# A Fourier mixing layer with a capped mixture of experts: when the first stage of two sequences runs, which engine copies it, and when its tables are asked for

## The chip, the core and the metric

The kernel runs on one core of a Trainium2 chip. The core has a matrix engine (TensorE, PE in the profile), VectorE (DVE), ScalarE (ACT), GpSimd (POOL), a queue engine (SyncE, SP) and 16 DMA engines that all transfers share. Each engine works through its own list of instructions in order, and waits for the others by semaphores. The metric is the time of one execution on the device, in microseconds (us); the figure for a kernel is the median of several executions. Before the change it is 474.11 us (three runs, 473.17 to 475.94).

## What is computed

Eight sequences of 2496 positions with 256 channels are filtered in the frequency domain, and the result goes through eight experts, each of which keeps at most 80 tokens:

```python
X = np.fft.rfft(x, axis=1)                       # x: (8, 2496, 256)
y = np.fft.irfft(X * (filt_r + 1j * filt_i)[None], n=2496, axis=1)
x = y.reshape(8 * 2496, 256)
logits = x @ w_gate                              # 8 experts
expert_idx = np.argmax(logits, axis=1)
# softmax probability of the chosen expert is the gate;
# of each expert's tokens the 80 with the largest gate are kept
out[tok_idx] = gate_w[tok_idx, None] * (np.maximum(x[tok_idx] @ w1[e], 0) @ w2[e])
```

All other rows of the output are zero.

## The kernel before

The Fourier transform is done by matrix products: 2496 is 39 times 64. The work of a sequence b runs in four stages.

- `stage1(b, k)`, k = 0 to 10 (L299 to L312), transforms over the 39. It reads one half of an x chunk (four row groups, 468 KB, `load_x`), makes eight PE instructions into one PSUM tile `pa` (pool `fps`, three buffers, shared with the next two stages), and copies 480 elements per partition into the tile `t1`, with a stride (L312). Eleven such units make a sequence. `t1` has two buffers, one for a sequence.
- `transpose1(b, u)`, u = 0 to 9 (L314), turns two slices of `t1` on PE and copies them with ScalarE into `t2` (L322).
- `stage2(b, u)` (L326) multiplies by the table `d_t` on PE (L331), by the filter on VectorE (two products, L339), and combines on GpSimd (two instructions, L345). It needs the piece `d(u // 2)` of the table and the filter row pair u in `ft`.
- `turn(b, u)` (L349) transforms over the 64 on PE, adds columns for the expert logits, copies the result with ScalarE (L369) and stores it.

The filter has to be brought into shape once: `load_filter(v, half)` (L265) issues two gathers of 128 KB from the GpSimd queue (half 0 the real part, half 1 the imaginary), `sign_filter(v)` (L273) flips signs in the imaginary part on ScalarE, and `turn_filter(v, k)` (L279) transposes on PE and copies with VectorE. There are five v of them, each for two values of u.

The order of all instructions is written out by hand. At the beginning seven x chunks are asked for on the SP queue (NX0 = 7 buffers; a sequence has NCH = 6 chunks), with the first table piece `load_d(0)` between the sixth and the seventh. GpSimd asks for the filter pieces (0, 0) and (0, 1), clears several tiles, copies two identities, and then executes a one-element copy `mark` that reads the last chunk of sequence 0 (L816); what stands behind it on GpSimd waits until that chunk is there. Behind it are four more filter pieces, (1, 0) to (2, 1), and two small pieces of the gate weights. On PE, `put_s1()` takes the next unit of stage 1 from a list over all sequences, and after every second one asks for one more x chunk (`put_x`), which waits for the buffer of the chunk just used. Eleven units are put first, then filter piece 0 is turned, then two transposes with a unit behind each. Then the loop at L853 runs over v = 10 b + u: stage2 of v, a piece of the filter (in the first eight steps), for v below 4 another `load_filter`, the transpose of v + 2, one unit of stage 1 (two at u = 3), and the turn of v - 2.

Of the kernel before, what the change touches and what calls it, by code (L numbers as in the profile page):

```python
# [27 lines left out]
NU = NS // 2  # L28

NJ, NG = 3, 22  # L30
NB = NG // 2
# [50 lines left out]
def kernel(  # L82
# [11 lines left out]
    nc = tc.nc  # L94
# [94 lines left out]
    def put_zeros(n):  # L189
        for i in zeros[:n]:  # L190
            nc.sync.dma_start(
                out=out[i * ZR:i * ZR + ZR, :].rearrange("r d -> (r d)").rearrange(
                    "(p m) -> p m", p=128),
                in_=zero_t[:])
        del zeros[:n]
# [36 lines left out]
    with ExitStack() as actx:  # L232
# [32 lines left out]
        def load_filter(v, half):  # L265
            k, filt = half, (filt_r, filt_i)[half]
            for i in range(2):
                nc.gpsimd.indirect_dma_start(
                    out=fst[:, v, 2 * k + i, :], out_offset=None, in_=filt[:, :],
                    in_offset=bass.IndirectOffsetOnAxis(  # L270
                        ap=frow[:, 2 * v + i:2 * v + i + 1], axis=0))

        def sign_filter(v):  # L273
            f = fst[:, v]
            for i in range(2):
                nc.scalar.activation(out=f[:, 2 + i, :], in_=f[:, 2 + i, :], func=AF.Copy,
                                     scale=fsig[:, 2 * v + i:2 * v + i + 1])
# [21 lines left out]
        def stage1(b, k):  # L299
            if k == 0:  # L300
                st["t1", b] = t1pool.tile([128, 4 * NS, N2], F32, name=f"t1_{b}", tag="t1")
            xt = st["x", b, 2 * k // JC]
            ps = fps.tile([128, 2, NJ, 4 * NS], F32, name=f"pa_{b}_{k}", tag="f")
            for i in range(2):
                for cb in range(NDB):
                    nc.tensor.matmul(  # L306
                        out=ps[:, i, :, 2 * NS * cb:2 * NS * cb + 2 * NS],
                        lhsT=xt[0:NJ * N1, (2 * k + i) % JC, 128 * cb:128 * cb + 128],
                        rhs=wf_t[:], start=True, stop=True)
            h = k // (NB - 1)  # L310
            t1 = st["t1", b][:, :, h:h + N2 - 1].rearrange("p a (j g) -> p g j a", j=NJ)
            nc.scalar.copy(out=t1[:, 2 * k - h:2 * k - h + 2], in_=ps[:])  # L312

        def transpose1(b, u):  # L314
            t1 = st["t1", b]
            ps = fps.tile([128, 2, NDB, 128], F32, name=f"pt_{b}_{u}", tag="f")
            for i in range(2):
                for cb in range(NDB):
                    a = 2 * NS * cb + 2 * (2 * u + i)
                    nc.tensor.transpose(ps[:, i, cb, :], t1[:, a:a + 2, :].rearrange("p r n -> p (r n)"), ident[:])  # L320
            t2 = t2pool.tile([128, 2, C], F32, name=f"t2_{b}_{u}", tag="t2")
            nc.scalar.copy(out=t2[:].rearrange("p i c -> p (i c)"),  # L322
                           in_=ps[:].rearrange("p i c q -> p (i c q)"))
            st["t2", b, u] = t2
# [456 lines left out]
        LATE, LEAD = 2, 2  # L781
        with tc.manual_schedule():
# [6 lines left out]
            def put_x():  # L789
                if xs:  # L790
                    load_x(*xs.pop(0))

            def put_s1():
                if s1:
                    b, k = s1.pop(0)
                    stage1(b, k)
                    if (2 * k + 2) % JC == 0 or k == NB - 1:
                        put_x()

            def load_d(g):  # L800
                nc.sync.dma_start(out=d_t[:, SG * g:SG * g + SG, :],
                                  in_=d_dram.ap()[:, SG * g:SG * g + SG, :])

            for _ in range(NCH):
                put_x()
            load_d(0)
            for _ in range(NX0 - NCH):
                put_x()
            load_filter(0, 0)
            load_filter(0, 1)  # L810
            for t in (lg, zero_t, *zs, key, kt):
                nc.gpsimd.memset(t[:], 0.0)
            nc.gpsimd.tensor_copy(out=gi[:, 0, E:E + 128], in_=ident[:])
            nc.gpsimd.tensor_copy(out=gi[:, 1, 0:128], in_=ident[:])
            mark = tpool.tile([1, 1], F32, name="mark")
            nc.gpsimd.tensor_copy(out=mark[:], in_=st["x", 0, NCH - 1][0:1, 0, 0:1])  # L816
            load_filter(1, 0)
            nc.gpsimd.dma_start(out=gi[:, 0, 0:E], in_=moe_w_gate[0:128, :])
            nc.gpsimd.dma_start(out=gi[:, 1, 128:128 + E], in_=moe_w_gate[128:256, :])
            load_filter(1, 1)  # L820
            load_filter(2, 0)
            load_filter(2, 1)
            for k in range(NB):
                put_s1()
                if k in (2, 5, 8):
                    load_d(k // 3 + 1)
            sign_filter(0)
            turn_filter(0, 0)
            turn_filter(0, 1)
            for v in range(LEAD):  # L830
                transpose1(0, v)
                put_s1()
            load_d(4)
            nlow = max(128 - cap, 8) // 8
            n0 = max(128 - cap, 8) // 8
            early = {67: [lambda: pick_edge(0, 6, 8, -1.0)],
# [16 lines left out]
            for v in range(B * NU + LATE):  # L853
                b, u = divmod(v, NU)
                if b < B:
                    stage2(b, u)
                    if v + 2 < NU:
                        if v % 2 == 1:
                            sign_filter(v // 2 + 1)
                        turn_filter(v // 2 + 1, v % 2)  # L860
                    if v < 4:
                        load_filter(3 + v // 2, v % 2)
                    elif v == 4:
                        nc.gpsimd.dma_start(out=e_t, in_=e_dram.ap())
                        nc.gpsimd.dma_start(out=wi_t, in_=wi_dram.ap())
                    w = v + LEAD
                    if w < B * NU:
                        transpose1(*divmod(w, NU))
                    put_s1()
                    if u == 3:  # L870
                        put_s1()
                    if b > 0:
                        put_zeros(1)
                if v >= LATE:
                    turn(*divmod(v - LATE, NU))
                if b > 0 and u == LATE:
                    logits(b - 1, 0)
                if b > 0 and b % 2 == 0:
                    if u == LATE + 1:
                        logits(b - 1, 1)  # L880
                    if b < 6 and u in (4, 5, 6, 7, 8, 9):
                        gating(b // 2 - 1, u - 4)
                        if u == 9:
                            gating(b // 2 - 1, 6)
                    elif b == 6 and u in (4, 5):
                        gating(2, 2 * u - 8)
                        gating(2, 2 * u - 7)
                    elif b == 6 and u in (6, 7):
                        gating(2, u - 2)
                        if u == 7:  # L890
                            gating(2, 6)
                for act in early.pop(v, []):
                    act()
                if v == B * NU:
                    turn_rows(0, 0)
                    turn_rows(0, 1)
# [656 lines left out]
```

## Time and profile before

The profile is of one execution.

| what | value |
|---|---|
| median of the runs | 474.11 us |
| the profiled execution | 481.94 us |
| its span, first to last instruction | 480.1 us |
| mean granted TensorE clock | 0.962 |
| PE busy | 442.1 us (92%) |
| weight loads of PE busy | 416.0 us (87%) |
| ACT busy | 222.4 us (46%) |
| DVE busy | 187.9 us (39%) |
| POOL busy | 176.6 us (37%) |
| copy of stage 1 (ACT, 88 of them) | 1000 ns each |
| copy after the transposes (ACT, 80) | 586 ns each |
| product with the filter (DVE, 160) | 681 ns each |
| combination (POOL, 160) | 735 ns each |
| gathers of the filter (POOL issues, 20) | about 950 ns each |

Busy time of an engine is time in which at least one of its instructions runs. Matrix instructions overlap, so PE's mean of one (about 275 ns) is more than the time by which each advances the engine. An entry such as "4.59 <-remote" behind an instruction says how long its engine stood idle before it, and what released it. The page cuts the span into 40 slices of 12 us; the opening that the change touches is the first five of them.

### The profile page before, as it was taken

The page shows a single profiled execution, that of the slowest core. Times are in us where ns is not written, and L with a number is a line of the kernel's source. Part 1 is how long each engine was busy: PE and PEld are TensorE (multiplying, and loading weights), DVE is VectorE, ACT ScalarE, POOL GpSimd, SP SyncE. Part 2 cuts the span into 40 slices and gives each one's busy share as a digit, 9 for nine tenths or more (in the row PEclk, how much of TensorE's full clock was granted, in tenths as well). Part 3 has the DMA queues.
Part 4 walks back from the last instruction along what each step waited for, and adds up shares of the span by engine and source line. Part 5 has one row for each costly group of instructions (what it writes and reads, how often), then busy time and mean ns, then how long its engine had stood idle before and what let it go on. Part 6 is the DMA issues. An engine that isn't in the chain of part 4 may idle for free. (4 is left out here: it accounts for less than half of the span.)

```text
span 480.1 us, 8658 instructions
## 1 busy us (share of the span) xinstructions
PE 442.1 (92%) x3372; PEld 416.0 (87%) x3372; DVE 187.9 (39%) x562; ACT 222.4 (46%) x364; POOL 176.6 (37%) x244
## 2 busy tenths in 40 slices
PE   5869999999999999999999987999889996999990
PEld 5769999999999999999999887888778886888870
DVE  2135553554664455655546995484110000011100
ACT  3835667666766666676667443322123220011110
POOL 7486434443543443444435446103620010211210
PEclk9979999999999999999999999999899996699996
DMA  7995467888778878788961326888779999155000
GB/s 215 279 293 167 151 192 218 246 262 251 250 247 254 268 271 248 203 265 280 401 238 47 132 89 213 311 338 324 283 268 383 379 389 349 53 181 173 20 18 11
DMA packets 38324, 109.95 MB, mean 229 GB/s; under 512 B 4667, under 2 KB 14202, under 8 KB 36760
## 3 DMA queue, kind: packets, MB, share of 16 engines
q1 hardware_dynamic: 26224, 73.26, 46.5%
q10 hardware_dynamic: 8642, 24.19, 13.1%
q0 software_dynamic: 3408, 11.86, 7.4%
q8 instruction: 29, 0.48, 0.4%
q14 instruction: 21, 0.17, 0.1%
HBM read 68.97 MB, written 43.20 MB: 234 GB/s over the span
## 5 line engine op out<-in xcount | busy, mean ns | idle before, releaser
L345 POOL TENSOR_TENSOR p<-p,p 128x256 f32<-128x256 f32 x160 | 114.0, 735 | 139.0 <-DVE p L339 97.2
L339 DVE TENSOR_TENSOR p<-pb,ft 128x512 f32<-128x512 f32 x160 | 102.3, 681 | 13.1 <-PE pb L331 10.7
L306 PE MATMUL pa<-wf_t,x 117*128 117x120 f32 x704 | 93.3, 280 | 6.6 <-DMA x<-in_x_dram 6.6
L312 ACT COPY t<-pa 128x480 f32<-128x480 f32 x88 | 87.0, 1000 | 26.4 <-PE pa L306 26.0
L306 PEld LDWEIGHTS pa<-wf_t,x 117*128 117x128 f32 x704 | 87.4, 197 | 6.9 <-DMA x<-in_x_dram 5.8
L354 PE MATMUL py<-gi,p 128*128 128x136 f32 x640 | 88.1, 280 | 1.3 <-POOL p L345 1.3
L331 PE MATMUL pb<-d_t,t 128*128 128x128 f32 x640 | 86.1, 278 | 0.9 <-DVE p L339 0.8
L354 PEld LDWEIGHTS py<-gi,p 128*128 128x128 f32 x640 | 79.8, 190 | 1.9 <-POOL p L345 1.9
L331 PEld LDWEIGHTS pb<-d_t,t 128*128 128x128 f32 x640 | 78.9, 193 | 1.7 <-DVE p L339 1.0
L322 ACT COPY t<-pt 128x512 f32<-128x512 f32 x80 | 46.9, 586 | 69.4 <-PE pt L320 64.8
L496 PE MATMUL po<-yb,wt 128*128 128x256 f32 x240 | 57.3, 383 | 2.0 <-ACT wt L489 2.0
L496 PEld LDWEIGHTS po<-yb,wt 128*128 128x128 f32 x240 | 43.8, 192 | 7.4 <-ACT wt L489 2.5
L320 PE MATMUL pt<-ident,t 128*128 128x128 f32 x320 | 48.5, 274 | 0.0
L489 ACT COPY wt<-pw 128x512 f32<-128x512 f32 x40 | 23.3, 586 | 54.1 <-PE pw L485 52.4
L374 DVE COPY z<-py 128x16 f32<-128x16 f32 x60 | 11.2, 186 | 91.9 <-ACT ysp L369 57.9
L320 PEld LDWEIGHTS pt<-ident,t 128*128 128x128 f32 x320 | 38.1, 143 | 0.0
L369 ACT COPY ysp<-py 128x512 f32<-128x512 f32 x60 | 35.4, 590 | 0.0
L1129 PEld LDWEIGHTS ph<-xs,w 128*128 128x128 f32 x256 | 32.9, 209 | 1.7 <-DVE xs L1120 1.2
L1129 PE MATMUL ph<-xs,w 128*128 128x80 f32 x256 | 33.1, 293 | 0.8 <-DVE xs L1120 0.8
L1144 PE MATMUL po<-w,hT 128*80 128x256 f32 x128 | 31.2, 402 | 0.0
L485 PE MATMUL pw<-ident,gts 128*128 128x128 f32 x160 | 24.7, 281 | 4.6 <-DMA gts<-rows_tbl,idxb 4.6
L1099 POOL DMA_INDIRECT xg<-y_sel,idxg x8 | 7.7, 962 | 55.9 <-ACT wt L489 40.3
(195 smaller groups left out, 315.7 us busy)
## 6 DMA issues: line engine op xcount, KB each, us to landing
out_dram<-zero_t SPq DMA_DIRECT2D x64, 312.0 KB
x<-in_x_dram SPq DMA_DIRECT2D x40, 468.0 KB
yf<-ysp ACTq DMA_DIRECT2D x30, 512.0 KB
yb<-yf SPq DMA_DIRECT2D x6, 2560.0 KB
w<-in_moe_w_dram SPq DMA_DIRECT2D x14, 1024.0 KB
yf<-ys ACTq DMA_DIRECT2D x10, 512.0 KB
w<-in_moe_w_dram ACTq DMA_DIRECT2D x2, 1024.0 KB
x<-in_x_dram SPq DMA_DIRECT2D x8, 234.0 KB
```

What stands on the lines that cost most here:

```text
L306: nc.tensor.matmul(out=ps[:, i, :, 2 * NS * cb:2 * NS * cb + 2 * NS], lhsT=xt[0:NJ * N1, (2 * k + i) % JC, 128 * cb:128 * cb + 128], rhs=w ...
L312: nc.scalar.copy(out=t1[:, 2 * k - h:2 * k - h + 2], in_=ps[:])
L320: nc.tensor.transpose(ps[:, i, cb, :], t1[:, a:a + 2, :].rearrange("p r n -> p (r n)"), ident[:])
L322: nc.scalar.copy(out=t2[:].rearrange("p i c -> p (i c)"), in_=ps[:].rearrange("p i c q -> p (i c q)"))
L331: nc.tensor.matmul(out=ps[:, cb, i], rhs=d_t[:, 2 * u + i, :], start=True, stop=True, lhsT=t2[:, i, 128 * cb:128 * cb + 128])
L339: nc.vector.tensor_tensor(out=pt, in0=ps[:].rearrange("p c s r q -> p (c s) r q"), in1=f.unsqueeze(2).to_broadcast([128, 2 * NDB, 2, NQ]), ...
L345: nc.gpsimd.tensor_tensor(out=yt[:, :, r, :], in0=yt[:, :, r, :], in1=pr[1][:, :, 1 - r, :], op=op)
L354: nc.tensor.matmul(out=ps[:, i, ZW * cb:ZW * cb + ZW], rhs=gi[:, cb, :], lhsT=yt[:, 2 * cb + i].rearrange("p r q -> p (r q)"), start=True, ...
L369: nc.scalar.copy(out=dst, in_=ps[:, :, E:E + C])
L496: nc.tensor.matmul(pos[t][:, 0, 0:C], lhsT=wts[t, g // 2][:, g % 2, i, :], rhs=ybs[t][:, s, :], start=(s == 0), stop=(s == NS - 1))
L1129: nc.tensor.matmul(ph[:, fc // 4, fc % 4, 0:cap], lhsT=self.w1s[e][:, k, 128 * fc:128 * fc + 128], rhs=xs[:, k, :], start=(k == 0), stop=( ...
L1144: nc.tensor.matmul(po[0:cap, :], lhsT=hT[:, fc, :], rhs=self.w2s[e][:, fc, :], start=(fc == 0), stop=(fc == NFC - 1))
```

## The change

Three things are moved in the opening. All 22 units of sequences 0 and 1 are put as one block before the filter is turned; the loop then puts no units for v = 0 to 7 and goes on as before from v = 8. For these two sequences the copy of a unit goes to VectorE where k is odd. The two filter pieces that GpSimd asked for first stand behind `mark` now, and the five table pieces are asked for during the second half of the block.

```diff
             h = k // (NB - 1)
             t1 = st["t1", b][:, :, h:h + N2 - 1].rearrange("p a (j g) -> p g j a", j=NJ)
-            nc.scalar.copy(out=t1[:, 2 * k - h:2 * k - h + 2], in_=ps[:])
+            copy = nc.vector.tensor_copy if b < 2 and k % 2 else nc.scalar.copy
+            copy(out=t1[:, 2 * k - h:2 * k - h + 2], in_=ps[:])
...
             for _ in range(NCH):
                 put_x()
-            load_d(0)
             for _ in range(NX0 - NCH):
                 put_x()
-            load_filter(0, 0)
-            load_filter(0, 1)
...
             nc.gpsimd.tensor_copy(out=mark[:], in_=st["x", 0, NCH - 1][0:1, 0, 0:1])
+            load_filter(0, 0)
+            load_filter(0, 1)
             load_filter(1, 0)
...
-            for k in range(NB):
+            for k in range(2 * NB):
                 put_s1()
-                if k in (2, 5, 8):
-                    load_d(k // 3 + 1)
+                if NB <= k < 2 * NB - 1 and k % 2:
+                    load_d(k // 2 - NB // 2)
             sign_filter(0)
             turn_filter(0, 0)
             turn_filter(0, 1)
             for v in range(LEAD):
                 transpose1(0, v)
-                put_s1()
-            load_d(4)
...
                     w = v + LEAD
                     if w < B * NU:
                         transpose1(*divmod(w, NU))
-                    put_s1()
-                    if u == 3:
+                    if v >= NU - LEAD:
                         put_s1()
+                        if u == 3:
+                            put_s1()
```

## The prediction, made before the changed kernel was run

> **What bounds the kernel now.** I read the page's slices first, then the stretches of the opening microseconds, then its timeline. Steps are called by their loop index v (one row pair of one sequence); "a unit" is one stage1 (two row groups). The page, one digit per 12 us:
>
> ```profile
> PE   5869999999999999999999987999889996999990
> ...
> PEclk9979999999999999999999999999899996699996
> DMA  7995467888778878788961326888779999155000
> ```
>
> TensorE is full from the fourth slice on. The change lies in the first five slices, where PE has holes, the clock falls once, and the DMA engines are near full for three slices. The answer by stretches (length, busy time of each engine with its instructions, granted clock, DMA share, GB/s):
>
> ```profile
> 13.30:18.80 5.50, 4.70 (x41) 4.55 (x41) 0.00 (x0) 4.41 (x6) 1.43 (x3) 1.00 0.88 264
> ...
> 27.90:31.40 3.50, 0.04 (x2) 0.02 (x1) 1.29 (x2) 1.83 (x4) 3.02 (x5) 0.85 0.93 297
> 31.40:37.20 5.80, 5.80 (x28) 5.70 (x29) 1.08 (x2) 1.90 (x3) 4.00 (x5) 0.50 0.86 261
> 37.20:61.00 23.80, 23.23 (x198) 22.07 (x198) 12.32 (x29) 15.96 (x25) 13.42 (x18) 1.00 0.48 152
> 60.00:260.00 200.00, 199.94 (x1767) 199.48 (x1766) 105.62 (x274) 135.25 (x205) 84.07 (x120) 1.00 0.77 249
> ```
>
> From 60 us on PE is busy 199.94 of 200 us: time won or lost before then reaches the end undiminished. The hole is one stall of 3.5 us and then 5.8 us at half clock. The timeline there, and around the first block:
>
> ```profile
> 5.78 7.54 PE L306 MATMUL pa<-wf_t,x 117*128 117x120 f32 x48 [5.78 <-DMA x<-in_x_dram]
> ...
> 13.78 2.02 PE L306 MATMUL pa<-wf_t,x 117*128 117x120 f32 x16 [0.46 <-DMA x<-in_x_dram]
> ...
> 16.14 2.91 PE L306 MATMUL pa<-wf_t,x 117*128 117x120 f32 x24 [0.34 <-DMA x<-in_x_dram]
> 16.91 0.18 POOL L816 COPY mark<-x 1x1 f32<-1x1 f32 x1 [5.77 <-DMA x<-in_x_dram]
> ...
> 26.86 1.06 PE L331 MATMUL pb<-d_t,t 128*128 128x128 f32 x8
> ...
> 28.28 1.41 POOL L345 TENSOR_TENSOR p<-p,p 128x256 f32<-128x256 f32 x2
> 29.57 0.59 ACT L322 COPY t<-pt 128x512 f32<-128x512 f32 x1 [4.59 <-remote]
> 29.76 1.29 DVE L339 TENSOR_TENSOR p<-pb,ft 128x512 f32<-128x512 f32 x2 [2.31 <-remote]
> ...
> 31.39 1.12 PE L284 MATMUL pf<-ident,fst 128*128 128x128 f32 x4 [3.46 <-ACT fst L276]
> ```
>
> PE waits for sign_filter on ScalarE, and ScalarE stood 4.6 us before a copy whose PE input, by PE's records, was finished at 26.14; VectorE stood too, though its input was finished at 27.92. "Remote" means no instruction of the trace explains the release. No other wait of the trace bears that name. So this stall isn't a dependency of the program.
>
> **What the Trainium skill says.** "TensorE: Matmul & The Clock Gate", What's actually happening: after an idle window of about 3.4 us the clock goes to half. The trace agrees: clock 0.50 right after 3.46 us of idleness, matmul groups 1.90 instead of 1.05 us. "DMA: Bandwidth & Descriptors", Issuing engines are not separate DMA queues: SP's and POOL's transfers share the same 16 engines and interleave. The trace agrees: 250 to 300 GB/s in total whether POOL's gathers run or not. "VectorE: DVE Perf Modes", the errata section's table: a PSUM copy costs 120 + elements cycles at 0.96 GHz, for 480 elements 0.63 us, an estimate; the nearest row here, VectorE's 128x512 PSUM copy, takes 0.69 us.
>
> **The change part by part.** Prices. The iterations at v = 8, 9 start their stage2 at 60.14 and 63.29: 3.15 us for 28 PE operations (stage2 8, transposes 4, stage1 8, turn 8), so 0.90 us for a unit, a stage2 or a turn, 0.45 for a transpose group or a filter turn. PE's work up to stage2 of v = 8 is the same before and after (22 units; thereafter the order is the same instruction for instruction). So I compare one moment: the start of stage2 at v = 8, 60.1 us in the profile.
>
> (1) Block of 22 units. The first six take until 13.3 as now (first x at 5.78, slow until the clock rises). Copies: ScalarE needs 1.00 us a unit, so alone it would hold PE (0.90) back; in turn with VectorE a pair needs 1.0 us against 1.8 of PE. VectorE's strided copy isn't in the trace: from 0.63 to about 1.2 us (ScalarE's strided 480 elements take 1.00, its 512 plain ones 0.59); either end is hidden, so 0. Sixteen units then give 13.3 + 14.4 = 27.7 at best.
>
> (2) Does x come in time? A chunk is 117 x 4 KB = 0.48 MB. Without gathers the x queue moves about 0.28 MB/us (279 and 295 GB/s at 15 to 21). Chunk 4 of sequence 0 landed at 16.14, when some 3.06 MB of that queue had moved (3.65 MB in all less 0.52 gathers and 0.07 small tables) though 2.40 were needed: later transfers interleave, so a chunk lands 0.6 MB late. Moving d(0) and the first four gathers away, chunks 3 and 4 land at about 11.9 and 13.6 (needed 13.3, 15.1) and chunk 5 at 14.5 (16.9 now). From there POOL gathers 128 KB each 1.25 us; their traffic begins about 2.5 us after issue, at 17, and leaves x 0.19 to 0.20 MB/us (total 0.29). At 17, 3.95 MB of 5.87 have moved (5.27 for two sequences, 0.6 late); the rest takes 9.6 us: last chunk at 26.6, just before its use at 26.8, with some 0.4 us lost on the chunk before. I take the block's end E at 28.1; bounds 27.7 and, at 0.17 MB/us, 29.2. SP's later entries x(2,0) and d(0) stand behind; d(0) lands near 30.3, needed at E + 3.4 = 31.5; d(1) needed 4 us later; 0.
>
> (3) POOL. The mark copy at 14.5 instead of 16.9, then 12 gathers x 1.25 + 1.2 for two small DMAs + 0.2: free at 30.9 (28.28 now). Its memsets move ahead from 7.6 to 2.7 us and wait for nothing. Behind the mark's wait for x stand all gathers and the two gate pieces; the filter turns wait for them, first at E, and sequence 0's first product at E + 5.8 = 33.9 finds POOL free: 0.
>
> (4) From E to stage2 of v = 0: turn_filter 0.45; sign_filter waits for ScalarE's last unit copy (1.0) and takes 0.9, so filter turns end at E + 2.2 (the same 2.2 as now between 18.8 and 21.03); two transposes 0.9; without the two units that now lie between, stage2 waits 0.3 for the ScalarE copy of 0.59. Start E + 3.4.
>
> (5) v = 0 to 7 without units. PE's own work: 1.8 each for v = 0 and 1, 2.7 each for six more; odd v lose 0.6 each to sign_filter, as now (the stage2 starts of v = 4 to 8 lie 3.58, 4.18, 3.59 and 4.17 apart). That gives v = 8 at E + 3.4 + 19.8 + 2.4 = E + 25.6. But POOL has 1.41 of products and two gathers (2.23, with gaps 2.44) for each of v = 0 to 3: 3.85 us a step. Its first product ends at E + 7.2 (stage2 0.9, VectorE 1.3, POOL 1.4, latencies), the fifth at E + 7.2 + 4 x 3.85 = E + 22.6, while PE would want it at E + 21.5. The units covered this until now. PE waits about 1.1, shared by v = 5 and v = 6: v = 8 at E + 26.7 = 54.8 us.
>
> Sum: 54.8 against 60.1 in the profile is -5.3 us. But the profiled execution took 481.9 us (span 480.1), 7.8 above the median 474.1, and the stall is worth 3.0 (31.4 instead of 28.4, when the gather for sign_filter would be there, an estimate from its neighbours' landings) and 2.9 (half of 5.8): 5.9. Without it v = 8 stands at 54.2, and the change costs 54.8 - 54.2 = +0.6. I hold the stall for something of the profiled execution: it has no releaser in the program, and it fills most of the 7.8. The cost that replaces the gains: the gain in the block (1.25 us of x waits and copies at 13.3 to 19.05) goes to POOL's 1.1 and the uncovered 0.3 + 0.4.
>
> **Rivals.**
> A. No measurable change, as summed: 474.7; own range 472.8 to 476.8. For it: the "remote" rows and the gap to the median. Chance 0.50.
> B. The stall belongs to the kernel, and the timed runs have it too; units in a block remove it (PE then waits for nothing that is 3.4 us long). -4 to -5.3: about 469.3. For it: DMA share 0.93 to 0.96 through all of 18 to 31, which the change relieves nowhere but reorders. Against: the median. Chance 0.28.
> C. Slower, one mechanism: the filter gathers, now started together beside the second half of the block, starve x(1, 3..5). If x gets 0.15 instead of 0.20 MB/us from 17 us on, the last chunk lands at 29.8, PE idles some 2.6 us in the block, and with sign_filter's 1 us behind it a clock window falls empty: 6.8 us at half clock, 3.4 more. It decides from about 2 us of lateness; 477 without the clock, 480 with it. Against: the x queue kept 0.19 beside gathers between 27 and 36 us. Chance 0.22.
> VectorE as the bound is excluded: 2.34 us an iteration against 2.7.
>
> **How the numbers follow.** A measurement tells about 0.5%, 2.4 us, from no change. Faster: 0.85 of B and a little of A, 0.28. Slower: nine tenths of C and a tenth of A, 0.26. The rest, 0.46, the same. The range 469 to 477.5 leaves out the strongest part of B and the clock case of C.
>
> **What would show it.** In the changed profile: mark at 14 to 15 us; x waits under 1 us in units 12 to 22; block end 27.7 to 29; turn's matmuls waiting for POOL's products at v = 5 and 6; stage2 of v = 8 near 55; no 0.5 clock before 300 us. An end of the block after 30, or half clock before 60, is C; a timed gain over 3 us is B. If products don't hold PE, step 5 was too dear by 1.1.

## The result, and the profile after

The changed kernel takes 475.49 us (median of 20 runs, 471.3 to 481.29); the kernel before, run beside it, 474.50 us (20 runs, 470.89 to 477.71). The recorded ratio is 1.0106, with an interval from 1.0061 to 1.0151: slower, where no measurable change was forecast. A recorded ratio leaves out executions that are over 1.5% above the fastest of their kernel, which are many where times scatter (18 of the 22 of e17, 8 of the 11 of the kernel before beside e9 to e12), so the medians over all executions stand beside it and say more there. Here the medians are only 0.2% apart, and the times on record don't show how a ratio of 1.0106 comes of them, so the size of the loss in this comparison is uncertain. The changed kernel run again on chip 15 (e2, e14) is slower by 1.1 to 1.6% by either measure. The profiled execution took 476.66 us, its span is 474.9 us, its mean granted clock 0.975. Three rows of the changed kernel's page, by slices of 12 us:

```profile
PE   5988899999999999999999997999899997999990
...
PEclk9999999999999999999999999899899998799997
DMA  6899547887778887788962224697959999654000
```

The deep hole of the third slice is gone, and the clock doesn't fall in the opening. (The clock has no record before its first change, at 14.08 us here, and the views show it as full there; a unit's 1.71 us until then, against 0.90 after, shows that PE ran at half.) The stretches of the same profile (length, busy time of PE, weight loads, DVE, ACT and POOL with the instructions of each, granted clock, DMA share, GB/s):

```profile
5.30:14.10 8.80, 8.50 (x38) 8.21 (x39) 1.89 (x4) 1.95 (x2) 0.11 (x1) 1.00 0.83 278
14.10:31.00 16.90, 16.17 (x141) 15.78 (x141) 10.06 (x32) 8.82 (x9) 11.85 (x14) 1.00 0.93 252
31.00:34.40 3.40, 2.22 (x17) 1.55 (x15) 1.46 (x3) 2.27 (x5) 1.19 (x2) 1.00 0.97 263
34.40:59.40 25.00, 21.95 (x177) 19.93 (x178) 16.46 (x34) 11.31 (x22) 18.98 (x25) 1.00 0.73 216
59.40:260.00 200.60, 200.52 (x1773) 200.05 (x1772) 106.20 (x275) 135.44 (x204) 85.12 (x122) 1.00 0.75 245
```

The block is no longer stopped, yet it isn't short either: in its first 8.8 us PE does 38 instructions, fewer than five units, and the loop's 25 us hold 3 us of idle PE. The timeline of the same profile at the places that the prediction named:

```profile
5.30 3.77 PE L306 MATMUL pa<-wf_t,x 117*128 117x120 f32 x16 [5.30 <-DMA x<-in_x_dram]
...
9.10 0.97 DVE L313 COPY t<-pa 128x480 f32<-128x480 f32 x1 [9.10 <-PE pa L306]
9.37 7.85 PE L306 MATMUL pa<-wf_t,x 117*128 117x120 f32 x48 [0.30 <-DMA x<-in_x_dram]
...
15.91 0.18 POOL L814 COPY mark<-x 1x1 f32<-1x1 f32 x1 [10.50 <-DMA x<-in_x_dram]
...
28.03 3.04 PE L306 MATMUL pa<-wf_t,x 117*128 117x120 f32 x24 [0.49 <-DMA x<-in_x_dram]
...
34.44 1.16 PE L332 MATMUL pb<-d_t,t 128*128 128x128 f32 x8 [0.24 <-ACT t L323]
...
48.46 0.44 PE L284 MATMUL pf<-ident,fst 128*128 128x128 f32 x2 [1.70 <-DMA fst<-in_filt_r_dram,frow]
...
59.36 1.05 PE L332 MATMUL pb<-d_t,t 128*128 128x128 f32 x8
```

Stage2 of v = 8 starts at 59.36, where the sum had 54.8. Three terms make the 4.6 us. The clock rose at 14.08 us (9.84 before), so six units ended near 15.4 (the first eight, 64 instructions, end at 17.22, and two take 1.8), not at 13.3: 2.1. The other sixteen took 15.7 to the block's end at 31.07 instead of 14.8: 0.9, of which 0.49 is the wait for x. And the loop took 28.3 from there instead of 26.7, because a filter piece came 1.70 us late at v = 4: 1.6.

### The profile page after: what moved, and what is told of

Same layout as the page of the kernel before. It is cut to its first block, busy times and chain, and to the rows that moved or that the text cites. A ratio compares the mean times of both kernels' runs of the same rounds, so it can differ in the third digit from the quotient of the medians.

```text
span 474.9 us, 8658 instructions
## 1 busy us (share of the span) xinstructions
PE 441.2 (93%) x3372; PEld 414.9 (87%) x3372; DVE 196.9 (41%) x572; ACT 213.9 (45%) x354; POOL 176.1 (37%) x244
## 3 DMA queue, kind: packets, MB, share of 16 engines
q10 hardware_dynamic: 8642, 24.19, 13.2%
## 5 line engine op out<-in xcount | busy, mean ns | idle before, releaser
L313 ACT COPY t<-pa 128x480 f32<-128x480 f32 x78 | 77.6, 1001 | 33.9 <-PE pa L306 33.3
L1128 PE MATMUL ph<-xs,w 128*128 128x80 f32 x256 | 32.3, 289 | 0.8 <-DVE xs L1119 0.8
```

Source lines behind the costliest of these rows:

```text
L1128: nc.tensor.matmul(ph[:, fc // 4, fc % 4, 0:cap], lhsT=self.w1s[e][:, k, 128 * fc:128 * fc + 128], rhs=xs[:, k, :], start=(k == 0), stop=( ...
```

## The experiments

Three theories went in. **The profiled stall is an accident** of one execution (what the prediction held). **The engines are short of data**: x or the filter comes late because the gathers take DMA bandwidth. **G**: a long row of filter gathers on GpSimd, one right after the other, makes PE's signals reach the copying engines late, so that a finished PSUM tile waits to be copied and PE runs out of its three buffers. In what follows, a *late copy* is a copy that starts 1.5 us or more after PE's records show its tile finished, while the copying engine stands idle. All runs are summed up first; "block end" is PE's end of the 22nd unit, "v = 8" the start of stage2 there, and the last columns give the kernel before on the same chip and the ratio with its interval.

| run | chip | block end | v = 8 | median | before | ratio |
|---|---|---|---|---|---|---|
| e1 before | 15 | | 59.83 | 481.66 | 481.62 | 1.0005 [0.9978, 1.0031] |
| e2 after | 15 | 37.0 | 63.94 | 488.32 | 481.62 | 1.0163 [1.0113, 1.0213] |
| e3 before, warm-up | 15 | | 58.02 | 481.41 | 481.62 | 1.0008 [0.9986, 1.0029] |
| e4 after, warm-up | 15 | 41.5 | 68.41 | 488.98 | 481.62 | 1.0106 [1.0035, 1.0177] |
| e5 after, plain transfers | 7 | 31.9 | 58.58 | 478.98 | 480.66 | 0.9948 [0.9920, 0.9975] |
| e6 after, gathers behind the block | 7 | 29.8 | 67.69 | 487.05 | 480.66 | 1.0112 [1.0079, 1.0145] |
| e7 after, piece 0 first | 7 | 36.35 | 63.54 | 485.67 | 480.66 | 1.0114 [1.0073, 1.0156] |
| e8 after, spaced | 7 | 29.8 | 58.27 | 480.83 | 480.66 | 1.0014 [0.9984, 1.0044] |
| e9 before, spaced | 4 | | 56.14 | 476.31 | 473.63 | none |
| e10 before, spaced less | 4 | | 56.80 | 475.32 | 473.63 | 1.0112 [1.0022, 1.0202] |
| e11 before, piece 2 in the loop | 4 | | 59.73 | 478.06 | 473.63 | 1.0148 [0.9980, 1.0317] |
| e12 after, spaced, ScalarE alone | 4 | 29.9 | 59.46 | 477.49 | 473.63 | 1.0179 [1.0071, 1.0287] |
| e13 before | 15 | | 58.56 | 481.01 | 480.85 | 1.0016 [0.9995, 1.0037] |
| e14 after | 15 | 32.3 | 62.10 | 486.27 | 480.85 | 1.0137 [1.0100, 1.0174] |
| e15 before, spaced | 15 | | 58.67 | 480.17 | 480.85 | 0.9985 [0.9962, 1.0008] |
| e16 after, spaced | 15 | 29.3 | 58.32 | 480.65 | 480.85 | 1.0001 [0.9978, 1.0024] |
| e17 before, piece 1 early | 4 | | 53.93 | 472.53 | 473.93 | 0.9929 [0.9864, 0.9994] |
| e18 after, pieces 0, 1 early | 4 | 32.5 | 59.45 | 479.38 | 473.93 | 1.0127 [1.0009, 1.0246] |

### e1 to e4: both kernels again, and with a warm-up of PE

e1 and e2 run the two kernels as they are. e3 (before) and e4 (after) add eight products of a unit matrix (PE works on them from 1.42 to 5.20 us) ahead of the first unit:

```diff
+            hot = pkps.tile([128, 4, 128], F32, name="hot", tag="k")
+            for i in range(8):
+                nc.tensor.matmul(out=hot[:, i % 4], lhsT=ident[:], rhs=ident[:], start=True, stop=True)
             xs = [...]
```

> The kernel before, unchanged, profiled a second time. If the stall at 27.9 us in the first profile belongs to that one execution, as the prediction held, the profile now shows no wait released by 'remote', no half clock between 20 and 60 us, and stage2 of v = 8 starts near 54.2 us instead of 60.1. If the stall belongs to the kernel (rival B), it stands there again and v = 8 starts near 60. The time against itself: ratio 1.00, which shows how far two series of one kernel lie apart.

> The changed kernel, unchanged, profiled a second time. Theory 1 (the late rise of the PE clock at 14.1 us is an accident of when the clock's window begins): the clock rises at another moment, between 9 and 14 us, and the block's end and stage2 of v = 8 (31.0 and 59.4 us in the first profile) move by half of that difference, down to 28.9 and 57.3. Theory 2 (the late rise comes with the change, because the second x chunk makes PE pause inside the window): the clock rises at about 14 again, v = 8 at 59 to 59.5. Time: 0.4 to 1% over before in either.

> Before, with eight products of the identity with itself on PE ahead of the first x chunk (their output is read by nothing). If the slow clock at the start costs about half of 4 us here, the first six units end at 11 to 11.5 instead of 13.3 us, but x is then waited for, so at v = 8 only 0.5 to 1 us is gained: 0.0 to 0.2% faster than before.

> The changed kernel with the same eight products of the identity ahead of the first x chunk. Theory clock (3 of the 4.6 us by which v = 8 came later than predicted are the slow clock until 14.1 us): the block ends at 28 us, v = 8 starts at 56 to 56.5, and the time falls by 0.5% against the changed kernel. Rival (the block is held back by the arrival of x and by its copies, not by the clock): the block ends at 30 to 31 whatever the clock, v = 8 stays at 59.

The stall of the kernel before was there again in e1 (half clock from 28.1 to 34.9 us), and also in e3 and e13, all on chip 15, so it was no accident of one execution. The timeline of e1 (start, length, instruction, idle time before it):

```profile
25.98 0.98 ACT L312 COPY t<-pa 128x480 f32<-128x480 f32 x1 [2.33 <-remote]
...
29.62 1.29 DVE L339 TENSOR_TENSOR p<-pb,ft 128x512 f32<-128x512 f32 x2 [8.07 <-PE pa L306]
...
31.05 2.04 PE L331 MATMUL pb<-d_t,t 128*128 128x128 f32 x8 [2.64 <-DVE p L339]
```

The changed kernel showed the same thing where it hurts. Timeline of e2, PE's units and the copies:

```profile
12.87 0.18 POOL L814 COPY mark<-x 1x1 f32<-1x1 f32 x1 [7.45 <-DMA x<-in_x_dram]
...
15.94 3.02 PE L306 MATMUL pa<-wf_t,x 117*128 117x120 f32 x24 [0.18 <-issue]
...
19.00 0.96 ACT L313 COPY t<-pa 128x480 f32<-128x480 f32 x1 [3.11 <-PE pa L306]
20.02 1.15 PE L306 MATMUL pa<-wf_t,x 117*128 117x120 f32 x8 [1.05 <-issue]
...
21.86 0.96 DVE L313 COPY t<-pa 128x480 f32<-128x480 f32 x1 [4.04 <-PE pa L306]
22.01 1.78 ACT L313 COPY t<-pa 128x480 f32<-128x480 f32 x2 [2.04 <-PE pa L306]
22.87 7.42 PE L306 MATMUL pa<-wf_t,x 117*128 117x120 f32 x40 [1.70 <-issue]
```

The group at 15.94 is three units, finished at about 17.1, 18.0 and 19.0; their copies start at 19.00, 21.86 and 22.01, on engines that had stood idle for 2 to 4 us. PE goes on only when a copy has freed a buffer (20.02, 22.87; "issue" says that the view found no release just before), and from 21.7 to 28.6 it has half its clock. x isn't short: PE waited for no x in the block after the first chunk.

The trace also keeps the times at which the signals themselves were recorded. Where nothing disturbs, PE's signal stands 0.01 to 0.02 us behind its result (in the recorded profile of the changed kernel 20.40 and 20.41). In e2 the signals of the units finished at 17.09, 17.99 and 18.97 us stand at 18.98, 21.83 and 21.93, and their copies start 0.02 to 0.08 us behind them. In the recorded profile of the kernel before, the results of 26.14, 27.02 and 27.92 us have their signals at 29.55, 29.64 and 29.73. So the signal is late, and not the copying engine; such a release is what the view called "remote".

The warm-up did nothing of use: the clock rose at 10.69 (e3) and 12.85 us (e4), and e4's block ended at 41.5 us, by late copies, where 28 or 30 to 31 had been forecast. (e4's profile is of its longest execution, 493.0 us; only its late copies and its clock are used here.)

On the late rise of the clock, both theories of e2 have a part. In every profile the clock changes only on a grid of 3.41 us (in e2 at 11.50, 21.74 and 28.57, three steps and two apart), and the grid lies differently against the kernel's start each time. The first rise came at the end of the first step in which PE was busy for 0.99 of it or more; steps with 0.85 to 0.92 weren't enough. In the recorded profile of the changed kernel the wait of 0.30 us for the second x chunk fell into such a step, and the rise came one step later (stretches, the first number behind the length is PE's busy time):

```profile
7.24:10.66 3.42, 3.12 (x15) 2.83 (x15) 0.97 (x1) 0.98 (x1) 0.00 (x0) 1.00 0.82 272
10.66:14.08 3.42, 3.42 (x18) 3.42 (x18) 0.90 (x3) 0.97 (x1) 0.00 (x0) 1.00 0.85 276
```

### e5 to e8: which property of the gathers does it

e5 replaces each gather by a plain transfer of 128 KB on the same queue (the filter gets other rows than it should, so its output is another); e6 puts `mark` and all filter requests behind the block; e7 puts filter piece 0 back to where the kernel before has it; e8 lets GpSimd clear a tile of zeros once more, 1.2 us, after each half piece behind `mark`, so that no more than two gathers follow each other.

```diff
# e5
-                nc.gpsimd.indirect_dma_start(
...
+                nc.gpsimd.dma_start(out=fst[:, v, 2 * k + i, :],
+                                    in_=filt[128 * (2 * v + i) % 1024:128 * (2 * v + i) % 1024 + 128, :])
# e6: mark and all that GpSimd issues behind it follow this loop
             for k in range(2 * NB):
                 put_s1()
...
+            nc.gpsimd.tensor_copy(out=mark[:], in_=st["x", 1, NCH - 1][0:1, 0, 0:1])
# e7: ahead of the memsets again
+            load_filter(0, 0)
+            load_filter(0, 1)
             for t in (lg, zero_t, *zs, key, kt):
# e8: after each of the six
             load_filter(0, 0)
+            nc.gpsimd.memset(lg[:], 0.0)
```

> The changed kernel with every indirect gather of the filter replaced by a plain transfer of the same size from the same queue (128 consecutive filter rows, so the output is computed with other filter rows). Theory G (back-to-back gathers on GpSimd, beside full DMA engines, delay PE's semaphores, so that ScalarE and VectorE start a copy 2 to 5 us after PE has written its input): no copy starts more than 1.3 us after its input between 15 and 35 us, the block ends before 31 us, v = 8 starts at 57 or earlier, and the time falls to that of before or below. Rival D (it is the full DMA engines alone, whatever asks for the transfers): the late copies stay, block end 35 to 41.

> The changed kernel with the mark copy and all twelve filter gathers behind it put after the block: the mark reads the last x chunk of sequence 1. The gathers then start at about 24 to 25 us. Theory G: the block is free of late copies until about 27 us and ends by 29.5, but the late copies then stand behind it and the filter comes 9 us later than now, so v = 8 starts at 65 or later and the time is 1% over the changed kernel's. Rival D: late copies inside the block at 17 to 25 us all the same. Rival X (x chunks land late because the gathers take bandwidth): PE's waits for x inside the block go from 0.5 us to 0, which G expects too; only the late copies tell them apart.

> The changed kernel with filter pieces (0, 0) and (0, 1) asked for first on GpSimd again, as before the change: a run of eight gathers behind the mark instead of twelve. Theory G: late copies begin as late after the mark but end 5 us earlier, block end 2 to 4 us earlier than in the changed kernel of the same chip, time 0.3 to 0.8% below it. If the order of the filter pieces doesn't matter, the time is the changed kernel's within 0.3%.

> The changed kernel with a clearing of 1.2 us on GpSimd (a tile that is zero anyway) after each of the six filter pieces behind the mark, so that never more than two gathers follow each other. Theory G in its narrow form (the length of the unbroken run of gathers decides): no late copies, block end before 31. If the number of gathers in flight or the bytes decide, the late copies stay, and the end of the run moves from 30 to 37 us, so v = 8 starts 3 us later than in the changed kernel.

e5 had no late copy; its block ended at 31.9 after two real waits for x, as its timeline shows:

```profile
25.65 2.02 PE L304 MATMUL pa<-wf_t,x 117*128 117x120 f32 x16 [0.74 <-DMA x<-in_x_dram]
...
28.89 3.04 PE L304 MATMUL pa<-wf_t,x 117*128 117x120 f32 x24 [1.22 <-DMA x<-in_x_dram]
```

So the same bytes on the same queue cost x 1.96 us, which is rival C's starvation, and it makes no half clock. (The rhythm is another, though: GpSimd needs 0.54 us for a plain transfer instead of 0.95, issues the first eight within 4.5 us, and then stands for up to 3.1 us until earlier ones have landed.) e6 has no gather beside the block: end at 29.8 us. e8 has all of them there, spaced: 29.8 as well, and no late copy. Between these two, the bandwidth that the gathers take costs the block nothing to be seen. e6 then pays for its order, 7.3 us of waiting for the filter and half clock until 45.0. Theory G had expected late copies behind its block, and there are none: no signal there is more than 0.7 us late. In e7, with eight gathers behind `mark` instead of twelve (two, the pieces of the gate weights, then six in a row), late copies are back from 22.8 to 29.8 us; two rows of its view of waits (engine, line, waited for: us in total, times, longest):

```profile
ACT t L313 <- remote: 5.8, 1, 5.8
...
PE pa L306 <- ACT t L313: 3.5, 2, 3.1
```

ScalarE stood 5.8 us until PE's late signals came (28.77 to 28.95 us), and PE 3.1 us for ScalarE. The block end of 36.35 us is a miss for G too, which had forecast a gain of 2 to 4 us from the shorter row. e7 to e8 is 485.67 to 480.83 us with as many gathers, though in e7 four of them come earlier; the clean pair, with the spacing alone between them, is e2 or e14 and e16 below. G is what fits: the unbroken row counts, not its bytes. Whether it counts by its length, by its rate or by the number of gathers under way at a time was not separated.

### e9 to e12: spacing in the kernel before, and ScalarE alone

e9 spaces the four half pieces behind `mark` of the kernel before by 1.2 us, e10 by 0.6 us (a smaller tile). e11 asks for filter piece 2 in the loop. e12 is e8 with all copies on ScalarE.

```diff
# e9 (e10: zero_t in place of lg)
             load_filter(1, 0)
+            nc.gpsimd.memset(lg[:], 0.0)
# e11
-            load_filter(2, 0)
-            load_filter(2, 1)
...
-                    if v < 4:
-                        load_filter(3 + v // 2, v % 2)
+                    if v < 6:
+                        load_filter(2 + v // 2, v % 2)
# e12
-            copy = nc.vector.tensor_copy if b < 2 and k % 2 else nc.scalar.copy
+            copy = nc.scalar.copy
```

> Before, with a clearing of 1.2 us on GpSimd after each of the four filter pieces behind the mark copy. If the stall of the kernel before at 24 to 31 us is the same thing as the late copies in the changed kernel's block (theory G), it goes: no copy more than 1.3 us behind PE between 20 and 35 us, no half clock there, v = 8 at 55 to 56.5 us instead of 58 to 60, and the time falls by 0.5 to 1%. If the stall of before has another cause, it stays, and the time rises by up to 0.5% for the 4.8 us of clearings on GpSimd.

> The same with clearings of 0.6 us. Theory G with a share of time as its measure (GpSimd must issue gathers less than about four fifths of the time): between before and the kernel with 1.2 us, late copies shorter or fewer. If any other instruction between the pieces is enough: as good as 1.2 us and 1 us earlier at v = 8.

> Before, with the two halves of filter piece 2 asked for inside the loop (v = 0 and 1, the others two steps later), so that four gathers and not eight follow each other behind the mark. Theory G: no late copies; but piece 2 then comes late for its turn at v = 2, which costs 2 to 4 us there. Time between -0.5 and +0.3%.

> The changed kernel with the clearings of 1.2 us and with all 22 copies of the block on ScalarE. Prediction step 1: ScalarE alone needs 1.0 us a unit where PE needs 0.9, so the block ends 1.5 to 2 us later than in the same kernel with copies in turn (29.8 us), and the time rises by 0.3 to 0.5%. If VectorE's copies are worth nothing (x sets the pace): block end within 0.5 us.

These four came out on chip 4, on which the kernel before takes 473.6 us and not 481, and whose runs spread more. e9 and e10 have v = 8 at 56.1 and 56.8 us in their profiles, but their medians are 0.6 and 0.4% above that of the kernel before. Why is left open; the kernel before was not profiled on this chip, and from v = 8 to the end the same instructions took between 414.1 and 419.5 us in the chip's six profiles, a scatter in which such gains drown. e11 moved the wait: PE stood for filter piece 2 from 32.2 to 34.8 us. None of the four has more than four gathers in a row here; but a row of eight near 340 us, which every profile has, brings no late signal on this chip (last section), so the spacing had nothing to take away. e12 is clear. Its timeline:

```profile
11.66 14.83 PE L306 MATMUL pa<-wf_t,x 117*128 117x120 f32 x127
...
13.13 14.38 ACT L313 COPY t<-pa 128x480 f32<-128x480 f32 x16 [0.46 <-PE pa L306]
```

Sixteen copies in 14.38 us on ScalarE alone are 0.90 us each: they follow one another at PE's own pace of 0.90 a unit, although each is listed with 0.98 to 1.00 us. The block ended at 29.9, where e8, with the copies in turn, had 29.8 on another chip. No worth of dividing the copies between two engines is to be seen.

### e13 to e16: the four forms side by side on chip 15

The kernel before and the changed one, as they are and with the spacing of e9 and e8.

> Before, unchanged, beside the next three on one chip. If this chip shows late copies: as on the second chip, stall between 24 and 31 us, v = 8 at 58 to 60. If not: v = 8 at 54.5 to 56.5, and no half clock before 290 us.

> The changed kernel, unchanged. With late copies on this chip: block end 35 to 37 us, v = 8 at 63 to 64, 1.3 to 1.6% slower than before. Without: block end 29.5 to 31, v = 8 at 58 to 59.5, that is 2 to 4 us behind before (0.4 to 0.9%), and the cost is then the slow start of the block and the waits for the filter, not the semaphores.

> Before with the clearings of 1.2 us between the filter pieces. Theory G: with late copies on this chip it is 3 to 4 us faster than before in the opening (v = 8 at 56), without them 0 to 1 us slower. If the stall of before isn't the gathers' doing, v = 8 stays at 58 to 60 on a chip with late copies.

> The changed kernel with the clearings. Theory G: v = 8 at 58 to 58.5 us on any chip; 5 us ahead of the changed kernel where there are late copies, within 1 us of it where there are none.

The same stretch of the block, first e2 (unbroken), then e16 (spaced), both from 17 us on:

```profile
17.00:32.00 15.00, 10.54 (x65) 9.98 (x64) 3.55 (x5) 4.44 (x5) 9.80 (x11) 0.77 0.89 266
```

```profile
17.00:29.30 12.30, 11.71 (x106) 11.56 (x105) 5.78 (x6) 6.75 (x7) 10.75 (x13) 1.00 0.93 275
```

At the same 266 to 275 GB/s, PE did 65 instructions in 15 us unbroken and 106 in 12.3 us spaced, and kept its clock. e14 had late copies from 21 to 32 us again, and half clock behind the block; e16 had neither. Spaced, the changed kernel is level with the one before (1.0001), unbroken it isn't (1.0137).

In the kernel *before* the spacing brought nothing. e15 had no late copy either, and stalled all the same:

```profile
28.07 1.18 POOL L824 MEMSET lg<- 128x1280 f32 x1
...
30.22 0.51 ACT L276 ACTIVATE fst<-fst,fsig 128x256 f32<-128x256 f32 x1 [1.40 <-DMA fst<-in_filt_i_dram,frow]
30.78 0.67 PE L284 MATMUL pf<-ident,fst 128*128 128x128 f32 x2 [2.09 <-ACT fst L276]
```

The first half of the imaginary part of filter piece 1 landed at 30.2 us and the second at 31.1; ScalarE's flip of signs waited for them and PE for ScalarE. But the spacing itself put them off: GpSimd issued the second half at 23.53 us, in e13 at 21.83. e11 shows the same order without the spacing and without late copies, with that gather at 21.74:

```profile
28.95 0.51 ACT L276 ACTIVATE fst<-fst,fsig 128x256 f32<-128x256 f32 x1 [0.48 <-DMA fst<-in_filt_i_dram,frow]
...
31.11 1.06 PE L331 MATMUL pb<-d_t,t 128*128 128x128 f32 x8
```

The second line is stage2 of v = 2. It starts at 31.11 us in e11 and at 34.37 in e13 (34.48 in e15), and from there to v = 8 both e13 and e15 take 24.19 us. So e15 exchanged one cause for another: it shows that a late filter piece can stop PE there, and not that the piece is as late in the kernel before. By e11, which ran on another chip, the late copies with their half clock cost the kernel before some 3.3 us on chip 15, an estimate from these starts (e11 also has fewer gathers under way).

### e17 and e18: bring the filter earlier

Asking for filter piece 1 ahead of `mark` should take away what is left of the wait for it, and it breaks the row as well: four gathers stay behind `mark`. e17 does only this. e18 does it in the changed kernel, for pieces 0 and 1.

```diff
# e17
+            load_filter(1, 0)
+            load_filter(1, 1)
             mark = tpool.tile([1, 1], F32, name="mark")
...
-            load_filter(1, 0)
...
-            load_filter(1, 1)
# e18: the same, and load_filter(0, 0), (0, 1) back ahead of the memsets
```

> Before, with filter piece 1 (four gathers) asked for ahead of the mark copy, where GpSimd waits for x from 11 to 17 us; four gathers are left behind the mark. If the filter's arrival sets the stall: PE's wait at 28 to 31 us and the half clock after it go, the first block ends 1 to 2 us later (x shares the DMA engines), v = 8 at 55.5 to 57 instead of 58.5 to 59.8, time 0.4 to 0.8% below before. If the semaphores set it: no late copies here either (a run of four), same gain; a stall that stays would speak against both.

> The changed kernel with filter pieces 0 and 1 ahead of the mark and four gathers behind it. Theory G: no late copies in the block (runs of four), but x comes later: eight gathers are 1.05 MB, 3.6 us at 0.29 MB/us, so PE waits for x and the block ends at 30 to 32 us; filter pieces 2 to 4 come 10 us earlier, so no wait for them; v = 8 at 57 to 58.5, equal to the spaced form within 0.3% and 1% ahead of the changed kernel on a chip with late copies.

The timeline and then the stretches of e17:

```profile
27.20 0.89 ACT L276 ACTIVATE fst<-fst,fsig 128x256 f32<-128x256 f32 x2
27.74 0.84 PE L284 MATMUL pf<-ident,fst 128*128 128x128 f32 x4 [0.48 <-ACT fst L276]
```

```profile
27.30:30.80 3.50, 3.06 (x26) 2.87 (x27) 1.98 (x3) 2.23 (x5) 3.03 (x5) 1.00 0.91 267
30.80:53.90 23.10, 22.52 (x192) 21.37 (x191) 12.68 (x28) 15.27 (x25) 15.56 (x21) 1.00 0.75 237
```

ScalarE no longer waits, PE waits 0.48 us where it waited 3.46 in the recorded profile of before, the clock stays at 1.00, stage2 of v = 2 starts at 29.74 us (31.11 in e11, so the filter piece accounts for some 1.4), and v = 8 at 53.93. As the edit takes away both causes at once, it can't tell them apart by itself. A gain in time isn't shown: the ratio of 0.9929 rests on 4 of 22 executions, and the medians, 472.53 and 473.93 us, are 0.3% apart on the chip whose runs spread most. e18 gains nothing: the gathers ahead of `mark` now take bandwidth from x, PE waited 2.7 us for it in the block, and the end came at 32.5.

## Why the prediction was wrong

**Two steps failed.** In the recorded profile it is the sum for the start of stage2 at v = 8, E + 26.7 = 54.8 us: it starts at 59.36, and the 4.6 us are terms of steps 1, 2 and 5 that were mis-sized (2.1, 0.9 and 1.6), listed below. On chips 15 and 7 it is, before that, the reading "so this stall isn't a dependency of the program". It set the rows "remote" aside as "something of the profiled execution". They were the signature of late copies, which came back in e1, e3 and e13, and the question to ask was what else they would hit: a block of 22 units, each of which needs a copy to free one of three PSUM buffers, put beside the longest row of gathers of all. In e2 that cost the block 37.0 minus 29.3 us of e16, half clock included. The stall *had* a releaser in the program: PE's own signal, 1.8 to 3.4 us behind its result. Without late copies PE still waits there for the filter piece, more briefly (e11).

By the traces, late copies go with the chip. That the stall "fills most of the 7.8" us between the profile and the median was a coincidence: the kernel before takes 480.7 to 481.6 us on chips 15 and 7 and 473.6 to 473.9 on chip 4, and on chip 15 profile and median agree (e13: 480.48 and 481.01). Which chips the recorded runs had isn't on record, but the traces bear marks. In chip 4's six profiles every recorded signal of PE in the opening stands 0.01 to 0.02 us behind its result, and of the 4000 records of landed transfers that a trace should hold they keep 3891 to 3901; the profiles of chips 15 and 7 keep 3421 to 3726. The recorded profile of before has late signals and 3491 records, that of the changed kernel no late signal and 3897. So the prediction probably read a profile of a chip like 15 beside a median of a chip like 4, and the recorded profile of the changed kernel, with two rows of six gathers and no late copy, is probably of one like 4.

**Rival C** named the right place, on chips 15 and 7 the right outcome (block end after 30, half clock, 1 to 1.6 per cent slower), and the wrong mechanism: in the block PE waited for x 0 us in e2 behind the first chunk, and 0.8 us in the recorded profile; with plain transfers of as many bytes it waited 1.96 us (e5), and lost no clock by it. Its test, "an end of the block after 30, or half clock before 60, is C", couldn't tell its mechanism from another with the same end.

**The terms of the sum.** In the recorded profile, which shows no late copy, v = 8 comes 4.6 us after the forecast by sizes alone. That the measured 475.49 us lies in the range of 469 to 477.5 all the same is luck: the sum missed the opening by 4.6 us, and the range, 8.5 us wide for other reasons, took that in.

- Step 1 took the clock's rise from one execution (9.84 us). In the changed kernel and its forms it came at 9.51 (e16) to 14.08 us, and each microsecond of delay costs PE half of one (1.71 instead of 0.90 us a unit). Mis-sized by 2.1.
- Step 2, block end 28.1: 29.3 at best (e16: clock at 9.51, one wait for x of 0.59), 31.07 in the recorded profile. Beside x, the constants that VectorE computes once are placed behind its first copies in the changed kernel and held unit 8 by 0.6 in e8.
- Step 3: `mark` at 12.87 and 15.91, forecast 14.5; right within the scatter.
- Step 4, E + 3.4: 34.44 minus 31.07 is 3.37. Right.
- Step 5, E + 26.7: 26.9 in e2 and in e18, with PE waiting 0.8 us once for POOL's product where 1.1 was forecast. Right where the filter is there. Where it isn't (28.3 recorded; 28.5 and 29.0 in e8 and e16, whose spacing delays it further), it was mis-sized: the filter turns' own wait for the later gathers was costed at 0, and the recorded profile has 1.70 us of it at v = 4.
- The kernel before without its stall: 54.2 forecast. e17, with its filter piece asked for earlier, reached 53.93; with the piece as it is, e11's 31.11 for v = 2 and the 24.19 us from there to v = 8 give 55.3, an estimate. On a chip like 4 the change then costs the opening some 4 us (59.36 against 55.3, an estimate too) where 0.6 was forecast. On chip 15 the timed runs do have the stall: v = 8 at 59.83 and 58.56 in e1 and e13.
- "Time won or lost before then reaches the end undiminished": from v = 8 to the end the profiles take 414.1 to 422.8 us with the same instructions, so a difference of a few microseconds in the opening needs many executions to show.
- VectorE's copy, bounded at 0.63 to 1.2 us, takes 0.96 to 1.04 and is hidden, as said. The gain on the copies that step 1 saw in the alternation isn't one (e12).

On chip 15 the kernel before loses some 3 to 5 us by its stall (58.56 and 59.83, against the 55.3 just estimated), and the changed one more by late copies (62.10 and 63.94, against 58.32 spaced). On chip 4 forms of the changed order reached v = 8 at 59.45 and 59.46, and forms of the old one at 53.93 to 56.80 (59.73 in e11, where filter piece 2 was asked for later): there the units in the loop seem to cover waits that the block leaves bare. **What stays open**: what inside the chip delays the signal and why only on some chips, and how large the loss on the chip of the recorded comparison really is. Nor is it settled whether the recording has a part in it, as all profiles with late signals lack records; the times of e2 and e14 against e16 show the loss over all executions.

## What to carry to other kernels

An unexplained release in a trace is a finding to test with a second profile, not an accident to subtract; ask what the planned change would put in its way. A gap between a profiled execution and a median says little until both are known to be of one chip. Where a profile shows late copies, a long row of gathers from GpSimd is worth breaking up by other work (e2 and e14 to e16), and work that needs a signal for every PSUM buffer shouldn't lie beside it. Small units between steps with waits can be cover, and taking them out for a dense block can bare the waits behind them.

## What the runs showed of the hardware

- Signals of PE can come 1.5 to 5 us late, several being released one behind the other, about 0.1 us apart. On chips 15 and 7 this was in every profile with six or more filter gathers in a row beside the units, beginning some 4 to 9 us after the first one and ending about 2 us after the last; it was in none with 1.2 us of other GpSimd work after every two, nor with plain transfers. In the opening of chip 4's profiles, with rows of two and four, and of the changed kernel's recorded one, with rows of six, no signal of PE is over 0.02 us late. ScalarE's and VectorE's own signals, where recorded, were late in no profile.
- The same occurs far from the change, in the profile of the kernel before, where a row of eight gathers (337.8 to 346.7 us) is followed by a ninth; PE's signals there stand at 350.65 to 350.81 us. Every profile of chips 15 and 7 has signals over 1.1 us late at this row, spaced forms too, and none of chip 4's, which have the same row. First the kernel before, then e11:

```profile
350.72 1.07 ACT L489 COPY wt<-pw 128x512 f32<-128x512 f32 x2 [5.15 <-PE pw L485]
351.36 1.99 PE L496 MATMUL po<-yb,wt 128*128 128x256 f32 x8 [2.00 <-ACT wt L489]
```

```profile
348.83 0.60 PE L485 MATMUL pw<-ident,gts 128*128 128x128 f32 x4
...
349.47 0.58 ACT L489 COPY wt<-pw 128x512 f32<-128x512 f32 x1 [1.65 <-PE pw L485]
```

- The Trainium skill, "TensorE: Matmul & The Clock Gate", What's actually happening, has the clock fall after an idle window of about 3.4 us. Here it fell with work in that window. In e2 it fell at 21.74 us, when the longest pause had been 1.05 us and PE had worked 1.79 of the 3.41 us before; in the recorded profile of the kernel before it fell at 30.32, within the pause of 3.46 us and not behind it, and PE had worked 1.02 of the 3.42 us before:

```profile
18.33:21.74 3.41, 1.79 (x14) 1.42 (x13) 0.00 (x0) 0.96 (x1) 2.98 (x4) 1.00 0.92 246
```

```profile
26.90:30.32 3.42, 1.02 (x10) 0.83 (x8) 1.11 (x2) 0.75 (x2) 2.94 (x5) 1.00 0.95 313
```

  The measurement decides. In the openings of all profiles the clock fell after each step of the grid with PE busy for less than 0.46 of it, and of the steps with 0.47 to 0.55 only after e2's.
- Eight small products ahead of the first unit didn't bring the clock's rise forward (10.69 and 12.85 us against 9.84 and 14.08 without).
- Chips differ by as much as the change does at most: the kernel before takes 473.6 to 473.9 us on chip 4 and 480.7 to 481.6 on chips 7 and 15, 1.5% more.
